# Attention and two feed-forward layers on one core: the hash codes' PSUM bank, maxima two slots earlier, weights in quarters

## The chip, the core and the metric

The kernel runs on one NeuronCore of a Trainium2 chip as a single program. The metric is device time in microseconds (us), the median of several executions. Engines are named as the profile names them: PE is the matrix engine (PEld its weight loads), DVE the vector engine, ACT the scalar engine, POOL GpSimd, SP the engine whose queue issues nearly all transfers.

## What is computed

Sixteen attention heads (2 batches of 8, 768 tokens, 64 columns each) in which a query sees only the keys with its own 6-bit hash code, then two layers over 1536 tokens of width 512 with 2048 hidden units.

```python
q_bits = (einsum('bhsd,dk->bhsk', q, proj) > 0); k_bits likewise
mask = q_bucket[:, :, :, None] == k_bucket[:, :, None, :]
scores = where(mask, scale * q @ k.T, -1e9)
attn = exp(scores - max(scores)); attn = attn / (sum(attn) + 1e-09)
x = (attn @ v) laid out as (1536, 512)
x = (mish(x @ w_in)) @ w_out
h = x @ w_in2;  P = a0 + a1*h + a2*h2 + a3*h3;  Q = 1 + |b0|*|h| + |b1|*h2
out = (P / (Q + 1e-06)) @ w_out2
```

## The kernel before

**Stages.** Attention comes first, head by head; the two layers follow (`moe`), whose matmuls on PE run without a break. What the change touches is all in `attention`.

**Slots.** Attention is written out by hand as a list of slots, six to a head: slot 6h + c holds, in the order of the table `order` (L506 to L533), every step due there. A row of the table is a name, a function, an offset and a count per head; `smax` at -9 means that the maxima of head h are taken from slot 6h - 9 on, one block c of 128 tokens in each slot. Steps before slot 0 are listed in `start` (L567), and steps after the last head are done within the first layer by `tail`. Every engine carries out its own instructions in this written order, so one that waits holds up all behind it on its engine; the same holds for the transfers that SP issues.

**A head's steps.** `load` brings k and q (`kq`, 64 rows each). `hi` (ACT) rounds them to the matrix engine's short format in `qB`, `lo` puts the remainder in `qX`, on POOL for even heads and DVE for odd ones. `move_k` copies k by a transfer (384 KB) from `qB` into both halves of `KK`. `move_x` issues two transfers, the second of which overwrites what the first reads, so SP waits in between. `codes` multiplies by the hash projection into a PSUM tile `cp`; `code_k` (DVE) and then `code_q` (ACT) turn it into 32 rows of `KK` and of `qB`. `code_q` overwrites rows of `qB` that `move_k` and `lo` read, so it waits for both. `smax` multiplies and takes each row's maximum on DVE (`mp`, L335); `fin_a` (three small DVE operations) and `fin_b` (four small transfers, two from SP and two from POOL) put the maxima back into `qB` as rows 29 to 31. `st` makes the scores (`sp`) and their exponentials `e` (ACT, L374). `pv` (`pv`) and `dsum` (`dn`) accumulate numerators and denominators in slots 3, 5 and 7; `evac` and `devac` copy them out, `recip`, `spread`, `norm`, `xhi` and `xlo` divide and split the result for the layers.

**PSUM.** Pool `ps` has three tiles, shared by `sp`, `mp`, `cp` and a small `vsp`; each is taken again once its reader is done. `pv` and `dn` have a bank each.

**Weights.** Meanwhile DVE turns 64-bit weights into 32-bit ones (`convert`, L100 to L106), POOL and DVE split the first five blocks, and the results go to DRAM; `first` reads each of these five blocks back in one transfer of 1024 KB (L143) at slots 80, 68, 74, 50 and 56.

Of the kernel before, what the change touches and what calls it, by code (L numbers as in the profile page):

```python
# [9 lines left out]
F32 = mybir.dt.float32  # L10
# [3 lines left out]
ACT = mybir.ActivationFunctionType  # L14
# [4 lines left out]
B, H, S, D = 2, 8, 768, 64  # L19
NT, DM, DFF = B * S, H * D, 2048  # L20
# [5 lines left out]
NC = S // 128  # L26
BIG = 2.0 ** 40
NBITS = 6
EARLY, FIRST = 5, (80, 68, 74, 50, 56)
SPLIT1, HERE1, W_AT, W_LEAD = 5, 10, (1, 7, 13, 19, 21), 3  # L30
DVE_LO = (("lo", 0),)
ENG = dict(
    lo="pd", hi="aa", xhi="a", xlo="pp", whi="pppp", wlo="pdpp",
)
C_AT = 16
ROW = 29
# [8 lines left out]
def attention_moe_moe(ctx: ExitStack, tc: tile.TileContext, kq, v, proj2, cst, eye, w1, w2, ab, out):  # L45
    nc = tc.nc

    def pool(stack, name, bufs=1, **kw):
        return stack.enter_context(tc.tile_pool(name=name, bufs=bufs, **kw))
# [111 lines left out]
    def attention(actx, tctx):  # L161
# [3 lines left out]
        dr_p = pool(tctx, "dr", 2, space=bass.MemoryType.DRAM)  # L165
        ac = pool(actx, "ac")
        kq_p = pool(actx, "kq")
        e_p = pool(actx, "pe", 5)
        v_p = pool(actx, "vp")
        sm_p = pool(actx, "sm", 2)  # L170
        ring[0] = pool(actx, "ring0", RING[0])
        ps = pool(actx, "ps", 3, space=PSUM)
        pvp = pool(actx, "pv", 1, space=PSUM)
# [11 lines left out]
        KK = [kq_p.tile([128, 2, S], R32, tag=f"kk{i}", name=f"kk{i}") for i in range(4)]  # L185
# [20 lines left out]
        raws = {}  # L206
# [21 lines left out]
        def lo(h, fn=None):  # L228
            if 0 <= h < B * H:
                fn = fn or lo_of("lo", h)  # L230
                fn(qX[h % 4], raws[h], qB[h % 4])

        def move_k(h):
            if 0 <= h < B * H:
                nc.sync.dma_start(
                    out=f32(KK[h % 4])[64:128], in_=f32(qB[h % 4])[0:64].unsqueeze(1).broadcast_to((64, 2, S))
                )

        def move_x(h):
# [55 lines left out]
        ct = {}  # L295


        def codes(h):
            if not 0 <= h < B * H:
                return  # L300
            ct[h] = ps.tile([128, 2, 512], F32, tag="s", name="cp")[:, 0]
            both(ct[h], p_raw, raws[h], start=True, stop=True)

        def code_k(h):
# [96 lines left out]
        Rt = {}  # L401
# [26 lines left out]
        def recip(h):
            if not 0 <= h < B * H:
                return  # L430
            cs = Rt.pop(h)
            rc = cs_p.tile([24, 32], F32, tag="rc", name="rc")

# [42 lines left out]
        nh = B * H  # L476
# [10 lines left out]
        for n, p in enumerate(parts):  # L487
            i = n // 5 * 24 + W_AT[n % 5]
# [6 lines left out]
                    if f is fn:  # L495
                        fn(0, *p)

        def first(f):
            (slot_both if wide64 else slot_f32)(0, f, lambda f: wpool)
            if not wide64:  # L500
                for s in range(2):
                    slot_hi(0, f, s)
                    slot_lo(0, f, s, lo_pool)
# [1 line left out]

        order = (  # L506
            ("st", st, 0, 6),
            ("smax", smax, -9, 6),
            ("fin_a", fin_a, -3, 1),
            ("fin_b", fin_b, -3, 1),  # L510
            ("hi", hi, -16, 1),
            ("move_k", move_k, -16, 1),
            ("lo", lo, -15, 1),
            ("codes", codes, -13, 1),
            ("pv", pv, (3, 3, 5, 5, 7, 7), 6),
            ("dsum", dsum, (3, 3, 5, 5, 7, 7), 6),
            ("vsum", vsum, 1, 0),
            ("code_k", code_k, -13, 1),
            ("code_q", code_q, -13, 1),
            ("evac", evac, 7, 1),  # L520
            ("devac", devac, 7, 1),
            ("recip", recip, 10, 1),
            ("spread", spread, 11, 1),
            ("norm", norm, 20, 0),
            ("xhi", xhi, 21, 0),
            ("vred", vred, -3, 0),
            ("xlo", xlo, 22, 0),
            ("move_x", move_x, -9, 1),
            ("load", load, -31, 1),
            ("load_v", load_v, -8, 0),  # L530
            ("weights", weights, 0, -1),
            ("first", first, FIRST, -2),
        )  # L533
        last = 6 * nh + 3
        slots = {}
        done = set()
        for name, fn, at, per in order:
            if name == "first":
                todo = [(at[f], (f,)) for f in range(EARLY)]
            elif type(at) is tuple:  # L540
                todo = [(at[c] + 6 * h, (h, c)) for h in range(nh) for c in range(per)]
            elif per > 0:
# [24 lines left out]
        start = (  # L567
            ("load", 0), ("get", 0), ("get", 1), ("hi", 0), ("codes", 0), ("move_k", 0), ("load", 1),
            ("lo", 0), ("get", 2), ("code_q", 0), ("code_k", 0), ("move_x", 0), ("smax", 0, 0), ("load", 2),
            ("smax", 0, 1), ("hi", 1), ("smax", 0, 2), ("codes", 1), ("move_k", 1), ("lo", 1), ("smax", 0, 3),  # L570
            ("load_v", 0), ("code_q", 1), ("smax", 0, 4), ("smax", 0, 5), ("fin_a", 0), ("fin_b", 0), ("code_k", 1),
            ("load", 3), ("move_x", 1), ("hi", 2), ("smax", 1, 0), ("coef",), ("move_k", 2), ("smax", 1, 1),
        )
# [305 lines left out]
```

## Time and profile before

| what | us |
|---|---|
| median of 3 runs (838.44 to 840.56) | 840.41 |
| the profiled execution | 841.66 |
| its span, first to last instruction | 839.1 |
| first scores (head 0 begins) | 23.30 |
| first matmul of the layers | 310.8 |

PE is busy for 790.9 us of the span, DVE for 589.3, ACT for 417.7. Head h is taken here from its first score matmul to that of head h + 1: they begin at 23.30, 45.83, 62.73, 78.79, 95.75, 117.35, 133.58, 149.71, 165.99, 189.21, 206.74, 222.75, 241.06, 263.12, 283.58 and 296.82 us. In a window's row PEclk is the granted TensorE clock as a share of the full one: 1.00 is 2.4 GHz, and a stretch at 1.2 GHz pulls the mean down. In a timeline's row the time in brackets is how long the engine stood idle before, and what ended that. A matmul's length overlaps the next one's, so PE's pace is read from start to start.

### The profile page before, as it was taken

What the parts mean: (1) busy time and instruction counts of PE and PEld (TensorE: products, weight loads), DVE (VectorE), ACT (ScalarE), POOL (GpSimd) and SP (SyncE); (2) the same over time, 40 slices, a digit from 0 to 9 for tenths busy, and PEclk for the clock granted to TensorE, in tenths of its full rate; (3) what the DMA queues carried; (4) which work ended last, traced back from release to release, by engine and by line L of the source; (5) the groups of instructions that cost most, each with busy time, mean ns of one, the idle gap of its engine ahead of it and who ended that gap; (6) DMA issues with size and microseconds to landing.
All of it is one profiled execution on the core that took longest, in us unless ns stands there. A gap on an engine that the chain in (4) does not pass through costs nothing.

```text
span 839.1 us, 10890 instructions
## 1 busy us (share of the span) xinstructions
PE 790.9 (94%) x3760; PEld 579.9 (69%) x3760; DVE 589.3 (70%) x1075; ACT 417.7 (50%) x680; POOL 84.6 (10%) x119
## 2 busy tenths in 40 slices
PE   4889899978988899999999999999999999999998
PEld 2545455445544458888888888887788888888886
DVE  4666657765664637865665567756999898889886
ACT  2245355444534354432222233337887777667674
POOL 2330415322030210000000000000000000000000
PEclk9899899999989899999999999999999999999999
DMA  5556665667655436332454468851000010001001
GB/s 133 171 133 164 173 163 162 177 173 186 180 149 155 131 99 220 92 109 89 148 169 159 140 180 267 238 176 55 1 1 0 13 38 0 1 1 51 0 1 50
DMA packets 58903, 95.41 MB, mean 114 GB/s; under 512 B 20866, under 2 KB 29154, under 8 KB 58210
## 3 DMA queue, kind: packets, MB, share of 16 engines
q1 hardware_dynamic: 57826, 94.65, 39.2%
q8 instruction: 29, 0.48, 0.2%
q0 software_dynamic: 1024, 0.09, 0.1%
q14 instruction: 24, 0.20, 0.1%
HBM read 62.43 MB, written 19.45 MB: 98 GB/s over the span
## 4 chain that ended last, share of the span: by engine, by line
PE 79%; DVE 8%; DMA 7%; ACT 2%; issue 2%; SPq 2%; POOL 0%; ACTq 0%; DVEq 0%
PE h L624 30%; PE y L642 15%; PE y L644 15%; PE sp L369 6%; PE pv L281 6%; DMA r<-w 4%; PE mp L331 3%; PE dn L396 3%; DVE m L335 3%; DMA kk<-qX 2%; DVE kk L308 1%; PE cp L281 1%; ACT qB L317 1%; DVE rc L434 1%; SPq L219 1%
## 5 line engine op out<-in xcount | busy, mean ns | idle before, releaser
L624 PE MATMUL h<-xh,w 128*128 128x512 f32 x768 | 204.9, 389 | 0.0
L624 PEld LDWEIGHTS h<-xh,w 128*128 128x128 f32 x768 | 144.2, 188 | 30.6 <-issue 0.6
L335 DVE TENSOR_REDUCE m<-mp 128x1 f32<-128x768 f32 x96 | 89.8, 945 | 51.1 <-PE mp L331 50.7
L70 DVE TENSOR_TENSOR gl<-ep,gh 128x512 fp32r<-128x512 f32 x96 | 67.1, 699 | 72.5 <-ACT ep L668 71.7
L374 ACT ACTIVATE e<-sp 128x768 f32<-128x768 f32 x96 | 77.3, 810 | 66.9 <-PE sp L369 63.6
L667 ACT ACTIVATE gh<-h 128x512 fp32r<-128x512 f32 x48 | 28.7, 598 | 162.3 <-PE h L624 153.5
L624 PE MATMUL h<-xl,w 128*128 128x512 f32 x384 | 102.7, 389 | 0.0
L644 PE MATMUL y<-w,gh 128*128 128x512 f32 x384 | 96.3, 389 | 0.0
L642 PE MATMUL y<-gh,w 128*128 128x512 f32 x384 | 94.8, 389 | 0.0
L642 PEld LDWEIGHTS y<-gh,w 128*128 128x128 f32 x384 | 72.1, 188 | 15.0
L644 PEld LDWEIGHTS y<-w,gh 128*128 128x128 f32 x384 | 72.1, 188 | 14.9
L624 PEld LDWEIGHTS h<-xl,w 128*128 128x128 f32 x384 | 72.1, 188 | 15.0
L281 PE MATMUL pv<-e,vf 128*64 128x384 f32 x384 | 77.0, 525 | 0.0
L369 PE MATMUL sp<-qB,kk 128*128 128x384 f32 x192 | 58.3, 386 | 18.7 <-DMA qB<-stt 5.1
L331 PE MATMUL mp<-kk,qB 128*128 128x384 f32 x192 | 58.3, 392 | 14.0 <-DVE kk L308 7.6
L369 PEld LDWEIGHTS sp<-qB,kk 128*128 128x128 f32 x192 | 32.1, 197 | 51.8 <-issue 25.9
L100 DVE TENSOR_SCALAR t<-r 128x256 int32<-128x256 int32 (+1 forms) x108 | 33.8, 313 | 47.3 <-DMA r<-w 46.0
L331 PEld LDWEIGHTS mp<-kk,qB 128*128 128x128 f32 x192 | 36.4, 210 | 26.6 <-DVE m L335 10.2
L674 ACT ACTIVATE ep<-h 128x512 f32<-128x512 f32 x48 | 28.6, 595 | 52.3 <-PE h L624 52.3
L106 DVE SCALAR_TENSOR_TENSOR r<-r,t 128x256 int32<-128x256 int32 (+1 forms) x108 | 51.2, 474 | 4.2
L103 DVE SCALAR_TENSOR_TENSOR t<-r,t 128x256 int32<-128x256 int32 (+1 forms) x108 | 51.3, 475 | 3.7
L644 PE MATMUL y<-w,gl 128*128 128x512 f32 x192 | 53.3, 392 | 0.5 <-DVE gl L70 0.4
(78 smaller groups left out, 1049.7 us busy)
## 6 DMA issues: line engine op xcount, KB each, us to landing
r<-w SPq DMA_DIRECT2D x88, 256.0 KB
w<-w SPq DMA_DIRECT2D x21, 512.0 KB
r<-w SPq DMA_DIRECT2D x20, 512.0 KB
w<-r SPq DMA_DIRECT2D x64, 128.0 KB
w<-r SPq DMA_DIRECT2D x30, 256.0 KB
kq<-kq SPq DMA_DIRECT2D x16, 384.0 KB
kk<-qB SPq DMA_DIRECT2D x16, 384.0 KB
w<-w SPq DMA_DIRECT2D x5, 1024.0 KB
```

The lines of the kernel that those rows point to most:

```text
L70: nc.vector.tensor_tensor(out=o, in0=i, in1=f32(h), op=ALU.subtract)
L100: lambda: nc.vector.tensor_scalar(out=t, in0=r[:, :, 1], scalar1=3, scalar2=0x3FFFFFF8, op0=ALU.logical_shift_left, op1=ALU.bitwise_and),
L103: lambda: nc.vector.scalar_tensor_tensor(out=t, in0=r[:, :, 1], scalar=-0x40000000, in1=t, op0=ALU.bitwise_and, op1=ALU.bitwise_or),
L106: lambda: nc.vector.scalar_tensor_tensor(out=o, in0=r[:, :, 0], scalar=29, in1=t, op0=ALU.logical_shift_right, op1=ALU.bitwise_or),
L281: nc.tensor.matmul(out=o[64 * a:64 * a + 64, 0:HALF], lhsT=w, rhs=qhalf(x, a), start=start, stop=stop)
L331: nc.tensor.matmul(out=p[:, a, 0:HALF], lhsT=qB[h % 4][:, c * 128:(c + 1) * 128], rhs=qhalf(KK[h % 4][:, 0], a), start=True, stop=True,)
L335: nc.vector.tensor_reduce(out=mt[h][:, c:c + 1], in_=halves(p), op=ALU.max, axis=AX.XY)
L369: nc.tensor.matmul(out=p[:, a, 0:HALF], lhsT=kk[:, c * 128:(c + 1) * 128], rhs=qq[:, a * HALF:(a + 1) * HALF], start=(i == 0), stop=(i == 1),)
L374: nc.scalar.activation(out=wide(e), in_=halves(p), func=ACT.Exp, scale=1.0 / D ** 0.5)
L624: nc.tensor.matmul(out=p, lhsT=w[:, c * 128:(c + 1) * 128], rhs=x[:, c, :], start=(n == 0), stop=(n == 11))
L642: nc.tensor.matmul(out=y[m], lhsT=w[:, DM + m * 128:DM + (m + 1) * 128], rhs=g, **s)
L644: nc.tensor.matmul(out=y[m], lhsT=g[:, m * 128:(m + 1) * 128], rhs=w[:, DM:2 * DM], **s)
```

## The change

- `codes` takes its tile from the denominators' pool (tag `dn`) instead of `ps`, and moves from offset -13 to -16, with `code_k`; `code_q` goes to -15. For the bank to be free then, `dsum` does its first group in slot 5 together with the second, and the pool of exponentials `e` grows from 5 to 6.
- `smax` goes from -9 to -11, `fin_a` and `fin_b` from -3 to -5, `hi` and `lo` to -18, `move_k` to -17; head 1 has a denser plan of its own.
- `move_x` is cut into `move_x` (-14) and `move_h` (-12); `devac`, `recip` give their transfers to `gather` (one slot later) and `store` (one slot later); `spread`, `norm`, `xhi`, `xlo` follow one to two slots later.
- `lo` is on POOL for all heads, `xlo` on DVE.
- `first` reads each of the five blocks in four transfers of 256 KB, two slots apart. Conversions move by two slots, their loads are issued four slots ahead instead of three.
- For head 0, `khi` (ACT) makes both copies of k from `kq`; the transfer `move_k` is not issued there.

```diff
-EARLY, FIRST = 5, (80, 68, 74, 50, 56)
-SPLIT1, HERE1, W_AT, W_LEAD = 5, 10, (1, 7, 13, 19, 21), 3
+EARLY, FIRST = 5, (84, 68, 76, 52, 60)
+SPLIT1, HERE1, W_AT, W_LEAD = 5, 10, (3, 9, 15, 17, 21), 4
-    lo="pd", hi="aa", xhi="a", xlo="pp", whi="pppp", wlo="pdpp",
+    lo="pp", hi="aa", xhi="a", xlo="dd", whi="pppp", wlo="pdpp",
-        e_p = pool(actx, "pe", 5)
+        e_p = pool(actx, "pe", 6)
+        def khi(h, i):
+            nc.scalar.activation(out=KK[h % 4][64:128, i], in_=raws[h][0:64], func=ACT.Copy)
...
-            ct[h] = ps.tile([128, 2, 512], F32, tag="s", name="cp")[:, 0]
+            ct[h] = pvp.tile([128, 512], F32, tag="dn", name="cp")
...
+        def first(f, n):
+            if wide64:
+                if n == 0:
+                    slot(0, f, lambda f: wpool)
+                c = slice(n // 2 * DM, (n // 2 + 1) * DM)
+                nc.sync.dma_start(out=f32(W[0, f])[:, n % 2, c], in_=scr[0, f][:, n % 2, c])
...
-            ("smax", smax, -9, 6),
+            ("smax", smax, -11, 6),
...
-            ("codes", codes, -13, 1),
+            ("codes", codes, -16, 1),
...
-            ("dsum", dsum, (3, 3, 5, 5, 7, 7), 6),
+            ("dsum", dsum, (5, 5, 5, 5, 7, 7), 6),
```

What this does to the engines' programs shows at three places. First PE in head 1, before: `sp` are scores, `mp` maxima, `cp` codes, `pv` and `dn` numerators and denominators.

```order
L369 MATMUL sp<-qB_122,kk_130 128x384 x2
L369 MATMUL sp<-qX_126,kk_130 128x384 x2
L331 MATMUL mp<-kk_132,qB_124 128x384 x2
L281 MATMUL cp<-kq,pr 64x384 x2
L281 MATMUL pv<-e,vf_133 64x384 x4
L396 MATMUL dn<-e,ones 32x384 x4
L369 MATMUL sp<-qB_123,kk_131 128x384 x2
```

The codes stand in the head's last slot, just ahead of a `pv` group. Now the same head after the change, from its third slot to its fifth.

```order
L337 MATMUL mp<-kk_132,qB_124 128x384 x2
L287 MATMUL cp<-kq,pr 64x384 x2
L375 MATMUL sp<-qB_122,kk_130 128x384 x2
L375 MATMUL sp<-qX_126,kk_130 128x384 x2
L337 MATMUL mp<-kk_132,qB_124 128x384 x2
L293 MATMUL pv<-qB_122,vs_136 128x384 x2
L287 MATMUL pv<-e,vf_133 64x384 x4
L375 MATMUL sp<-qB_122,kk_130 128x384 x2
L375 MATMUL sp<-qX_126,kk_130 128x384 x2
L337 MATMUL mp<-kk_132,qB_124 128x384 x2
```

The codes now follow the third slot's maxima, the fourth slot's `pv` has no `dn` behind it, and the sixth slot ends with eight `dn` matmuls in the bank that the codes had.

Second, SP's queue in the same head, before: `kk<-qB` is `move_k`, `qB<-stt` is `fin_b`, `kk<-qX` and `qX<-qB` are `move_x`, `cs`, `d` and `R` belong to the division.

```order
L423 DMA cs<-dv 24x1x32 x2
L235 DMA kk_129<-qB_121 64x2x768
L138 DMA w_0_306<-r 128x512
L139 DMA w_0_306<-r 128x512
L355 DMA qB_123<-stt_117 3x6x32 x2
L241 DMA kk_132<-qX_128 64x768
L242 DMA qX_128<-qB_124 64x768
```

After the change the two transfers of `fin_b` come directly ahead of `move_k`:

```order
L248 DMA qX_128<-qB_124 64x768
L361 DMA qB_123<-stt_117 3x6x32 x2
L238 DMA kk_129<-qB_121 64x2x768
L435 DMA cs<-dv 24x1x32 x2
L244 DMA kk_129<-qX_125 64x768
L138 DMA w_0_364<-r 128x512
```

So `move_k` of head 4 stands on SP behind the maxima of head 2, which DVE has to finish first; `move_x` is no longer followed by the transfer that waits for it.

Third, ACT round `code_q` (L317 before, L323 after), before:

```order
L412 ACTIVATE ev<-pv 64x384 x2
L420 ACTIVATE dv<-dn 128x384
L374 ACTIVATE e<-sp 128x768
L61 ACTIVATE qB_121<-kq 128x768
L374 ACTIVATE e<-sp 128x768 x3
L317 ACTIVATE qB_121<-cp,cst 32x384 x2
```

and after:

```order
L61 ACTIVATE qB_121<-kq 128x768
L380 ACTIVATE e<-sp 128x768
L418 ACTIVATE ev<-pv 64x384 x2
L426 ACTIVATE dv<-dn 128x384
L380 ACTIVATE e<-sp 128x768 x2
L323 ACTIVATE qB_121<-cp,cst 32x384 x2
```

Between `hi` (L61) and `code_q` there were three exponentials' time; there are now three exponentials and the two copies `ev` and `dv`, and `move_k` starts a slot later.

## Rows read from the trace of the kernel before

**Rows 1.** Windows: stretch, length, busy per engine (count), PEclk, DMA share, GB/s.

```profile
23.30:45.83 22.53, 19.17 (x82) 12.00 (x83) 13.21 (x22) 7.19 (x10) 5.02 (x8) 0.85 0.60 166
45.83:95.75 49.92, 46.33 (x276) 25.76 (x273) 34.48 (x59) 24.67 (x38) 12.95 (x16) 1.00 0.60 162
95.75:117.35 21.60, 18.42 (x96) 9.90 (x92) 14.26 (x28) 8.50 (x13) 8.04 (x11) 0.84 0.51 140
117.35:165.99 48.64, 46.18 (x277) 25.70 (x273) 32.98 (x57) 25.58 (x40) 18.77 (x20) 1.00 0.67 178
165.99:283.58 117.59, 99.78 (x546) 54.68 (x542) 71.03 (x131) 50.61 (x77) 26.98 (x36) 0.93 0.64 166
283.58:310.80 27.22, 27.22 (x176) 14.47 (x172) 13.12 (x27) 13.68 (x22) 3.12 (x4) 1.00 0.36 114
310.80:839.08 528.28, 523.80 (x2308) 432.18 (x2304) 398.03 (x737) 281.38 (x474) 2.36 (x2) 1.00 0.28 87
```

**Rows 2.** Waits of PE, whole span: us in total, times, longest.

```profile
PE mp L331 <- DVE kk L308: 7.6, 2, 5.0
PE mp L331 <- DVE m L335: 6.3, 8, 1.8
PE cp L281 <- ACT e L374: 5.3, 10, 0.6
PE sp L369 <- DMA qB<-stt: 5.1, 3, 2.2
PE sp L369 <- ACT qB L317: 4.7, 3, 2.0
PE sp L369 <- DVE m L335: 4.3, 5, 1.1
```

**Rows 3.** Timeline of the start: start us, length, instruction, [idle before, releaser].

```profile
4.72 0.74 SPq L235 DMA_DIRECT2D kk<-qB  x1
...
8.69 1.16 ACT L317 ACTIVATE qB<-cp,cst 32x384 fp32r<-32x384 f32 x2 [3.99 <-DMA kk<-qB]
9.95 1.37 DVE L308 TENSOR_SCALAR kk<-cp,cst 32x384 fp32r<-32x384 f32 x2 [4.27 <-ACT qB L317]
...
10.72 2.63 PE L331 MATMUL mp<-kk,qB 128*128 128x384 f32 x6 [5.03 <-DVE kk L308]
...
12.67 0.62 SPq L235 DMA_DIRECT2D kk<-qB  x1
...
18.20 1.16 ACT L317 ACTIVATE qB<-cp,cst 32x384 fp32r<-32x384 f32 x2 [6.62 <-DMA kk<-qB]
...
23.30 0.98 PE L369 MATMUL sp<-qB,kk 128*128 128x384 f32 x2 [1.15 <-issue]
```

**Rows 4.** Timeline where head 8 begins: VectorE, GpSimd, ScalarE and PE.

```profile
163.62 1.83 POOL L67 TENSOR_TENSOR qX<-kq,qB 128x768 fp32r<-128x768 f32 x1
...
164.37 2.09 DVE L434 TENSOR_TENSOR rc<-cs 24x32 f32<-24x32 f32 x1
...
168.27 0.62 PE L331 MATMUL mp<-kk,qB 128*128 128x384 f32 x2 [1.30 <-DVE m L335]
...
170.87 1.01 PE L369 MATMUL sp<-qB,kk 128*128 128x384 f32 x2 [1.98 <-ACT qB L317]
```

**Rows 5.** Timeline round a weight transfer of 1024 KB, between heads 12 and 13.

```profile
253.69 1.25 SPq L143 DMA_DIRECT2D w<-w  x1
...
255.04 1.56 SPq L355 DMA_DIRECT2D qB<-stt  x2
...
263.12 0.59 PE L369 MATMUL sp<-qB,kk 128*128 128x384 f32 x2 [1.62 <-DMA qB<-stt]
```

**Rows 6.** Timeline of PE at the end of head 4, a quiet place.

```profile
114.48 0.87 PE L281 MATMUL cp<-kq,pr 128*64 128x384 f32 x4 [0.43 <-ACT e L374]
...
116.57 0.85 PE L396 MATMUL dn<-e,ones 128*32 128x384 f32 x8
...
117.35 0.62 PE L369 MATMUL sp<-qB,kk 128*128 128x384 f32 x2
```

More of the change, by code (lines that the diff above doesn't have):

```diff
@@ L241, in move_x, with move_h @@
                 nc.sync.dma_start(out=f32(KK[h % 4])[0:64, 1], in_=f32(qX[h % 4])[0:64])
+        def move_h(h):
+            if 0 <= h < B * H:
                 nc.sync.dma_start(out=f32(qX[h % 4])[0:64], in_=f32(qB[h % 4])[64:128])
@@ L420, in devac, with gather @@
             nc.scalar.activation(out=dv, in_=pvt.pop((h, "d"))[:, 0:HALF], func=ACT.Copy)
+            Rt[h] = dv
+        def gather(h):
+            if not 0 <= h < B * H:
+                return
+            dv = Rt.pop(h)
             cs = cs_p.tile([24, 2, 32], F32, tag="cs", name="cs")
@@ L439, in recip, with store @@
             nc.vector.reciprocal(out=rc, in_=rc)
+            Rt[h, "r"] = rc
+        def store(h):
+            if not 0 <= h < B * H:
+                return
+            rc = Rt.pop((h, "r"))
             d = dr_p.tile([24, 32], F32, tag="d", name="d")
@@ L496, in weights @@
                         fn(0, *p)
-        def first(f):
-            (slot_both if wide64 else slot_f32)(0, f, lambda f: wpool)
-            if not wide64:
+        def first(f, n):
[4 more added lines that the diff above has]
+                nc.sync.dma_start(out=f32(W[0, f])[:, n % 2, c], in_=scr[0, f][:, n % 2, c])
+            elif n == 3:
+                slot_f32(0, f, lambda f: wpool)
                 for s in range(2):
@@ L507, in attention @@
             ("st", st, 0, 6),
-            ("smax", smax, -9, 6),
[L509 to L513, printed above, removed]
-            ("codes", codes, -13, 1),
+            ("smax", smax, -11, 6),
+            ("fin_a", fin_a, -5, 1),
+            ("fin_b", fin_b, -5, 1),
+            ("hi", hi, -18, 1),
+            ("move_k", move_k, -17, 1),
+            ("lo", lo, -18, 1),
+            ("codes", codes, -16, 1),
             ("pv", pv, (3, 3, 5, 5, 7, 7), 6),
-            ("dsum", dsum, (3, 3, 5, 5, 7, 7), 6),
+            ("dsum", dsum, (5, 5, 5, 5, 7, 7), 6),
             ("vsum", vsum, 1, 0),
-            ("code_k", code_k, -13, 1),
-            ("code_q", code_q, -13, 1),
+            ("code_k", code_k, -16, 1),
+            ("code_q", code_q, -15, 1),
             ("evac", evac, 7, 1),
             ("devac", devac, 7, 1),
+            ("gather", gather, 8, 1),
             ("recip", recip, 10, 1),
[L523 to L528, printed above, removed]
+            ("store", store, 11, 1),
+            ("spread", spread, 12, 1),
+            ("norm", norm, 22, 0),
+            ("xhi", xhi, 23, 0),
+            ("xlo", xlo, 24, 0),
+            ("vred", vred, -5, 0),
+            ("move_x", move_x, -14, 1),
+            ("move_h", move_h, -12, 1),
             ("load", load, -31, 1),
-            ("load_v", load_v, -8, 0),
+            ("load_v", load_v, -10, 0),
             ("weights", weights, 0, -1),
@@ L538, in attention @@
             if name == "first":
-                todo = [(at[f], (f,)) for f in range(EARLY)]
+                todo = [(at[f] + 2 * n, (f, n)) for f in range(EARLY) for n in range(4)]
             elif type(at) is tuple:
                 todo = [(at[c] + 6 * h, (h, c)) for h in range(nh) for c in range(per)]
+            elif name == "smax":
+                todo = [(c // 2 if h == 1 else at + 6 * h + c, (h, c)) for h in range(nh) for c in range(per)]
+            elif name.startswith("fin_"):
+                todo = [(at + 6 * h + (h == 1), (h,)) for h in range(nh)]
             elif per > 0:
@@ L567, in attention @@
         start = (
[L568 to L572, printed above, removed]
+            ("load", 0), ("get", 0), ("get", 1), ("hi", 0), ("codes", 0), ("khi", 0, 0), ("lo", 0), ("load", 1),
+            ("code_q", 0), ("code_k", 0), ("khi", 0, 1), ("get", 2), ("move_x", 0), ("smax", 0, 0), ("hi", 1),
+            ("smax", 0, 1), ("move_k", 1), ("load", 2), ("lo", 1), ("smax", 0, 2), ("codes", 1), ("move_h", 0),
+            ("smax", 0, 3), ("smax", 0, 4), ("smax", 0, 5), ("fin_a", 0), ("fin_b", 0), ("code_k", 1), ("code_q", 1),
+            ("load_v", 0), ("move_x", 1), ("load", 3), ("hi", 2), ("move_k", 2), ("smax", 1, 0), ("coef",),
+            ("move_h", 1), ("smax", 1, 1),
         )
@@ L577, in run @@
             fns = {o[0]: o[1] for o in order}
-            fns.update(get=get, coef=coef)
+            fns.update(get=get, coef=coef, khi=khi)
             for name, *k in start:
-                done.add((name, tuple(k)))
+                done.add(("move_k" if name == "khi" else name, tuple(k[:1]) if name == "khi" else tuple(k)))
                 fns[name](*k, **({"fn": lo_dve} if (name, *k) in DVE_LO else {}))
@@ L585, in tail @@
         def tail(i):
-            for g in {1: range(last, last + 3), 3: range(last + 3, last + 6), 4: range(last + 6, last + 30)}.get(i, ()):
+            for g in {1: range(last, last + 3), 2: range(last + 3, last + 5), 4: range(last + 5, last + 30)}.get(i, ()):
                 slot_ops(g)
```

## The prediction

> **What bounds the kernel now.** I read the windows first. The layers take 528.28 us from their first matmul on, 523.80 of them with PE busy at a clock of 1.00 [rows 1]; no step of the change runs there except the ends of the last pair's division, so I carry this stretch over unchanged. The room is in the 310.8 us before it. There the heads differ: heads 5 to 7 take 48.64 us, 16.2 each, heads 1 to 3 take 16.6 each, but head 0 takes 22.5, head 4 takes 21.6, and heads 8 to 13 take 117.59, which is 19.6 each [rows 1]. All do the same work, so what they take above 16.2 is waiting and a lower clock: 6.3 + 1.3 + 5.4 + 20.4 = 33.4 us. The clock's part shows in PEclk: 0.84 over the 21.60 us of head 4 means (1 - 0.84)/0.5 x 21.6 = 6.9 us at 1.2 GHz instead of 2.4, which costs up to half of that, 3.5 us; every window with PEclk under 1.00 is one with long heads. Heads 14 and 15 (27.22 us) have next to no maxima or codes left to do.
>
> Next the waits of PE. Its six largest sums are 7.6, 6.3, 5.3, 5.1, 4.7 and 4.3 us, together 33.3 [rows 2]. The first belongs mostly to the start. PE, then, is the bound in the quiet heads, and in the others it stands behind short chains of other engines.
>
> Two places show these chains. Where head 8 begins, POOL's 1.83-us `lo` starts at 163.62; a DVE operation on only 24x32 elements that starts 0.75 us later takes 2.09 us; the maxima queue behind it on DVE, PE waits 1.30 us for one, the codes' readers come late too, and PE waits 1.98 us more because the tile that its next scores want still holds the codes (`ACT qB L317`) [rows 4]. Between heads 12 and 13, a transfer of 1024 KB is issued at 253.69, the maxima's two small ones 1.35 us later, and PE gets them only at 263.12, after a wait of 1.62 us [rows 5].
>
> **The change part by part.**
>
> *Start.* ACT stands idle for 3.99 us until 8.69 because `code_q` overwrites rows that the transfer `move_k` reads (issued at 4.72) [rows 3]. `khi` puts a pass of ACT over 768 columns there; the two passes of `code_q`, 384 columns each, take 1.16 together [rows 3], so I price it at 0.8 to 1.2. The wait shrinks by 2.8 to 3.2 us, and the second copy stands behind `code_q`, with no one waiting. `code_k` and the first maxima (10.72) follow as before. Term: -3.0. Head 0's scores then begin near 20.
>
> *Codes' bank.* `cp` no longer waits for an exponential (5.3 us in 10 waits) and scores no longer wait for `code_q` (4.7 us in 3) [rows 2]; in a quiet head this is the 0.43 before `cp` [rows 6]. The new wait is for `devac`, one slot earlier; it is the last of three ACT copies behind `pv` and `dn`, and has a slot's scores and maxima as cover. If that cover is gone it costs what it cost before, about half a microsecond a head. `cp` itself (114.48 to 115.18 with what follows, 0.70) only moves. The merged `dn` group is the same matmuls (0.78 from start to start [rows 6]) and go to the sum as they are.
>
> *Maxima two slots earlier.* The 5.1 us behind `qB<-stt` go: two slots are about a third of a head, 5.4 us, against a lateness of 1.62 in the case shown. What is late next is `code_q`, below.
>
> *Weights in quarters.* The 1024 KB that stood in front of small transfers becomes 256 KB at a time. Bounds: nothing, or all of what heads 8 to 13 have above the quiet ones. SP issues 15 transfers more; at 1.25 us, the longest row I have [rows 5], that is 19 us of a queue spread over six heads (96 us), and it is hidden as long as SP waits for others anyway.
>
> *`lo` to POOL, `xlo` to DVE; loads four slots ahead; `gather`, `store`, `move_h`.* Eight `lo` against seven or eight pairs' `xlo` is an exchange of equal size, off PE's path. The division's new place takes `recip` away from `lo`, so the case of rows 4 goes, and with it most of the 6.3 + 4.3 us behind DVE's maxima. But it puts `lo` of every head beside `fin_a`. The last pair's `norm` now ends two slots later, inside the first layer; the columns that it makes are first used 16 blocks in. A sixth `e` tile costs only memory.
>
> The Trainium skill ("SBUF — State Buffer", section "Who interferes with whom") says that DVE and GpSimd hold one pair of ports as an exclusive lock for a whole instruction, and that the later one fully blocks. The 2.09 us of rows 4 agree in kind. By this rule `fin_a` (operations from SBUF to SBUF) would wait for the rest of each `lo`, at most its 1.83 us, per head; that is a delay on the chain priced next, and no wait of PE by itself.
>
> *The new chain.* `code_q` waits for `move_k` to land, and `move_k` now stands behind `fin_b` on SP, which stands behind `fin_a`. From issue to `code_q`'s start it took 3.97 us (4.72 to 8.69) and 5.53 (12.67 to 18.20) [rows 3]. Behind it, `code_q` takes 1.16, then `dn` may have its bank. So the chain from `fin_a` is 1.56 for two issues [rows 5], 4.0 to 5.5, and 1.16: 6.7 to 8.3 us, or up to 10.1 with a `lo` of 1.83 in front. From the second slot, where it begins, to the sixth, where `dn` wants the bank, are four of six slots, 4/6 x 16.2 = 10.8 us. So it just fits: I take no wait in most heads. In the two heads where a weight's split stands in the same slot on POOL and SP, `move_k` is delayed by it further, and I expect a wait of 1.5 to 2 us and a stretch of low clock (3.5) each, some 10 us in all. Queued behind `code_q` on ACT are the exponentials of slots 4 and 5, for which the next head's first scores wait.
>
> *Sum.* Start -3.0. Head 0, denser than before, 20.5 instead of 22.5: -2.0. Heads 1 to 13 at 15.7 (16.2 less the 0.53 of one `cp` wait): 13 x 15.7 = 204, plus the 10 us of new waits, 214, against 49.92 + 21.60 + 48.64 + 117.59 = 237.8: -23.7. Heads 14 and 15 and the layers: 0. Together -28.7, so the profiled execution's 841.66 would be 813.0. It stands 1.25 us above the median of the runs shown (840.41); from that median the forecast is 811.7, and I say **812 us**.
>
> **Range of the forecast's own case.** Without the 10 us and with head 0 at 17.5, -42: 798. With half of the excess of heads 8 to 13 left (10) on top of the new waits, -19: 822.
>
> **The rivals.**
>
> *Only the bank and the start* (disturbed heads stay). The unknown is whether quarters and earlier maxima cure heads 8 to 13. For: the same number of bytes still passes, beside the same loads. Against: each long wait there had a named cause that the change moves away. It keeps 3.0 + 5.3 + 4.7 = 13 us, so 827; with the wait for maxima also gone, 822.
>
> *The new chain is late in every head* (slower). If `move_k` needs more than 10.8 - 1.83 - 1.56 - 1.16 = 6.2 us from issue to landing, PE waits at `dn` in each head, ACT's exponentials follow late, and the clock falls. Price: a wait of 2 us in 13 heads and a low stretch of 3.5 after every second, 26 + 24 = 50 us, against 38.7 that are gained without new waits: +11, so 852. It decides from 38.7/13 = 3.0 us a head on. For it: the sum of the longest rows fits by 0.7 us only, and weights' quarters pass at the same time. Against: the other row, 3.97, leaves 2.2.
>
> *The bank is not free* (the change doesn't do what it says). `cp` waits for `devac` as it waited for the exponential. Then heads 1 to 13 stay at 16.2: 6.9 us less, 819.
>
> **How the numbers follow.** Forecast's case 0.62 (798 to 822), only bank and start 0.16, bank not free 0.08, a chain late in some heads that eats nearly all of the gain 0.05 (about 840), late in all 0.09. Within 0.3%, which is 2.5 us and about what a measurement of this kernel can tell from no change, lies the fourth. Faster by more 0.86, same 0.05, slower 0.09. The range leaves out the two last cases and a little at the low end: 799 to 831.
>
> **What would show it.** Right: first scores near 20 us; no row in which PE's `cp` waits for `e` or `sp` for `code_q`; heads 8 to 13 under 17 us each; at most two or three stretches at the low clock. Wrong: PE's `dn` waiting for ACT's `code_q`, and ACT's `code_q` for the transfer `kk<-qB`, in many heads; the last `fin_a` operation stretched to the end of POOL's `qX` and PE behind it; PE idle in the first blocks of the layers, because a weight's last quarter or the last division comes late.

## The result

| kernel | median, us | ratio to before | 95% interval |
|---|---|---|---|
| before | 839.42 | | |
| changed | 808.93 (808.24 to 808.95, 4 runs) | 0.9636 | 0.9616 to 0.9656 |

The forecast was 812, with 799 to 831. The kernel before and its variants scatter by about 1% either way, so for them I go by the ratio, which leaves disturbed runs out; the changed kernel's runs agree within 0.1%.

The profile after, windows over the same groups of heads as [rows 1] (stretch, length, busy per engine with counts, PEclk, DMA share, GB/s):

```profile
19.78:44.14 24.36, 19.77 (x88) 11.83 (x87) 15.05 (x24) 7.91 (x11) 8.47 (x9) 0.77 0.79 200
44.14:92.66 48.52, 45.75 (x276) 25.97 (x272) 37.63 (x63) 24.77 (x38) 17.93 (x21) 1.00 0.66 177
92.66:108.72 16.06, 15.62 (x97) 8.73 (x93) 13.67 (x24) 8.16 (x13) 5.06 (x5) 1.00 0.64 169
108.72:156.32 47.60, 46.03 (x276) 25.89 (x272) 38.60 (x64) 24.87 (x39) 20.76 (x23) 1.00 0.71 189
156.32:251.05 94.73, 91.38 (x546) 51.77 (x542) 70.85 (x127) 50.13 (x78) 22.57 (x26) 1.00 0.68 187
251.05:277.16 26.11, 26.11 (x172) 14.04 (x168) 12.01 (x29) 13.59 (x22) 1.32 (x2) 1.00 0.51 150
277.16:806.90 529.74, 524.08 (x2308) 432.11 (x2304) 397.78 (x739) 281.89 (x474) 0.00 (x0) 1.00 0.28 87
```

Head 4 takes 16.06 us where it took 21.60; heads 8 to 13 take 94.73 instead of 117.59, and PEclk is 1.00 in every window from head 1 on. Of these stretches of heads only head 0's has become longer, 24.36 instead of 22.53, at a PEclk of 0.77. Put into the prediction's sum:

| term | forecast | measured | from |
|---|---|---|---|
| start, to the first scores | -3.0 | -3.5 | 23.30 to 19.78 |
| head 0 | -2.0 | +1.8 | 22.53 to 24.36 |
| heads 1 to 13 | -23.7 | -30.8 | 237.75 to 206.91 |
| heads 14 and 15 | 0 | -1.1 | 27.22 to 26.11 |
| layers | 0 | +1.5 | 528.28 to 529.74 |
| sum | -28.7 | -32.2 | span 839.08 to 806.90 |

The waits of PE, of ACT and of DVE on which the rest turns (us in total, times, longest):

```profile
PE mp L337 <- ACT qB L323: 6.5, 2, 4.1
PE mp L337 <- DVE m L341: 5.7, 11, 1.5
PE mp L337 <- DVE kk L314: 2.3, 1, 2.3
PE dn L402 <- ACT qB L323: 0.3, 1, 0.3
...
ACT qB L323 <- DMA kk<-qB: 25.3, 11, 4.1
...
DVE t L100 <- DMA r<-w: 18.7, 13, 4.3
```

Of [rows 2], the lines in which `cp` waits for `e`, `sp` for `code_q` and `sp` for `qB<-stt` are gone. The new chain is there, as the ACT line shows: `code_q` stands behind `move_k`'s transfer 11 times for 25.3 us. But PE pays 0.3 us for it at `dn`, once; the 6.5 us before `mp` lie ahead of head 0's first scores and in head 0 (below).

So the total came out, and the symptom that it rested on (long heads become quiet ones) is what happened. Which part of the change does it, the prediction had argued only from single waits. That is what the experiments ask.

### The profile page after: what moved, and what is told of

It is laid out like the page before. It is cut to its first block, busy times and chain, and to the rows that moved or that the text cites. A ratio compares the mean times of both kernels' runs of the same rounds, so it can differ in the third digit from the quotient of the medians.

```text
span 806.9 us, 10904 instructions
## 1 busy us (share of the span) xinstructions
PE 778.0 (96%) x3760; PEld 575.8 (71%) x3760; DVE 595.3 (74%) x1083; ACT 419.1 (52%) x682; POOL 83.7 (10%) x111
## 3 DMA queue, kind: packets, MB, share of 16 engines
q0 software_dynamic: 1024, 0.09, 0.1%
## 4 chain that ended last, share of the span: by engine, by line
PE 78%; DVE 12%; DMA 2%; ACT 2%; issue 1%; SPq 0%; POOL 0%; DVEq 0%; ACTq 0%; POOLq 0%
PE h L656 29%; PE y L676 15%; PE y L674 14%; PE pv L287 6%; PE sp L375 6%; PE dn L402 4%; DVE m L341 4%; PE mp L337 3%; DMA r<-w 2%; DVE w L70 1%; DVE kk L314 1%; DVE t L103 1%; DVE xl L70 1%; DVE r L106 1%; DVE t L100 1%
## 5 line engine op out<-in xcount | busy, mean ns | idle before, releaser
L699 ACT ACTIVATE gh<-h 128x512 fp32r<-128x512 f32 x48 | 28.7, 598 | 150.8 <-PE h L656 141.8
L287 PE MATMUL pv<-e,vf 128*64 128x384 f32 x384 | 72.5, 499 | 0.0
L337 PE MATMUL mp<-kk,qB 128*128 128x384 f32 x192 | 55.7, 381 | 16.6 <-ACT qB L323 6.5
L375 PE MATMUL sp<-qB,kk 128*128 128x384 f32 x192 | 56.6, 376 | 0.5 <-ACT e L380 0.5
L708 DVE TENSOR_TENSOR n<-n,ep 128x512 f32<-128x512 f32 x48 | 33.1, 690 | 26.7 <-ACT n L707 26.7
```

The costliest lines, as they stand in the source:

```text
L337: nc.tensor.matmul(out=p[:, a, 0:HALF], lhsT=qB[h % 4][:, c * 128:(c + 1) * 128], rhs=qhalf(KK[h % 4][:, 0], a), start=True, stop=True,)
L375: nc.tensor.matmul(out=p[:, a, 0:HALF], lhsT=kk[:, c * 128:(c + 1) * 128], rhs=qq[:, a * HALF:(a + 1) * HALF], start=(i == 0), stop=(i == 1),)
L708: nc.vector.tensor_tensor(out=v_, in0=v_, in1=u, op=ALU.mult)
```

## The experiments

First the changed kernel with single parts undone. Three undo kernels that change nothing measurable (below) gave 808.15 to 808.28 us, and the changed kernel itself 808.93, so I take 808.5 us as the reference for all of them.

### Weights in one transfer each

```diff
-                if n == 0:
-                    slot(0, f, lambda f: wpool)
-                c = slice(n // 2 * DM, (n // 2 + 1) * DM)
-                nc.sync.dma_start(out=f32(W[0, f])[:, n % 2, c], in_=scr[0, f][:, n % 2, c])
+                if n == 0:
+                    slot_both(0, f, lambda f: wpool)
```

> The changed kernel (808.9 us), but each of the five weight blocks comes back in one transfer of 1024 KB, at the slot where its first quarter stood. Theory (quarters carry a part of their own): move_k, now 3.5 to 3.8 us from issue to landing in the middle heads, lands behind 1024 KB only after 6 to 8 us in the heads that have such a transfer; code_q follows late, PE waits at dn or mp, and the clock falls in some of them: 6 to 15 us slower (815 to 824), the excess in heads 8 to 15. Rival (the earlier maxima give enough slack by themselves, the quarters are not needed): late landings show on SP and ACT, but PE hardly waits: 807 to 811.

Measured: 808.28 us (808.21 to 808.65), ratio 0.9666 (0.9625 to 0.9708). The rival holds: cutting the blocks is worth nothing.

### Maxima back at their old place

```diff
-            ("smax", smax, -11, 6),
-            ("fin_a", fin_a, -5, 1),
-            ("fin_b", fin_b, -5, 1),
+            ("smax", smax, -9, 6),
+            ("fin_a", fin_a, -3, 1),
+            ("fin_b", fin_b, -3, 1),
```

> The changed kernel, but the maxima at -9 and fin_a, fin_b at -3 as before. Theory (the quarters already cured the late maxima): fin_b lands 1.9 to 2.9 us after its issue now and has three slots, about 8 us, before the scores want it, so PE waits for qB<-stt nowhere, and the time is 807 to 811. Rival (the two slots carry the gain of heads 8 to 13): the 5.1 us of waits behind qB<-stt come back with one to three stretches of low clock, 815 to 824.

Measured: 808.26 us (807.89 to 809.6), ratio 0.9668 (0.9626 to 0.9711). No scores wait for `qB<-stt` anywhere. The earlier maxima are not needed either.

### Both of these undone at once

> The changed kernel with both undone at once: weight blocks in one transfer each, and the maxima at -9 with fin_a, fin_b at -3. Each alone left the time at 808.3. Theory A (each covers for the other: early maxima stand the long transfer, quarters let late maxima pass): undone together, the waits for qB<-stt of before come back in heads 8 to 13, with low clock, 814 to 822. Theory B (neither carries anything; what disturbed heads 4 and 8 to 13 was the codes in the pool ps and lo beside recip): 806.5 to 811.

Measured: 808.15 us (807.55 to 809.22), ratio 0.9623 (0.9592 to 0.9653). They don't cover for each other; theory B holds against theory A. One reservation: the blocks stand here in the new slots. Before, all five stood one slot ahead of `fin_b`, and in its trace POOL's small transfers issued 1.4 to 3.2 us behind a block landed 5.5 to 7.2 us after their issue, all others in 1.7 to 4.0. In this kernel only one block stands there. But the place isn't needed either: a kernel below (the one before with bank and conversions) has the blocks whole and in their old slots and the maxima at -9, and in it too no scores wait for `qB<-stt`.

### Codes back in the pool of the scores

```diff
-            ct[h] = pvp.tile([128, 512], F32, tag="dn", name="cp")
+            ct[h] = ps.tile([128, 2, 512], F32, tag="s", name="cp")[:, 0]
```

> The changed kernel, but the codes take their tile from the pool ps again, in the new slots. Theory (the bank carries about 10 us): scores and maxima wait again until code_q has read the tile, and code_q now waits for move_k in most heads, so the waits are longer than the 5.3 + 4.7 us of before: 10 to 25 us slower, 819 to 834, with PE rows sp or mp waiting for code_q. Rival (the bank only moves a wait): within 2.5 us, 806.5 to 811.5.

Measured: 818.87 us (818.83 to 820.65), ratio 0.9799 (0.9748 to 0.9851), 10.4 us slower than the reference, at the low end of what the theory said. PE's waits in this kernel:

```profile
PE sp L375 <- DVE m L341: 7.7, 7, 1.4
...
PE sp L375 <- ACT qB L323: 5.5, 6, 1.1
```

Scores wait for `code_q` again, six times, and for maxima whose tiles come free later; neither row exists after the change. The clock stays at 1.00 in heads 1 to 13, which take 215.78 us instead of 206.91.

### `lo` and `xlo` back on their engines

```diff
-    lo="pp", hi="aa", xhi="a", xlo="dd", whi="pppp", wlo="pdpp",
+    lo="pd", hi="aa", xhi="a", xlo="pp", whi="pppp", wlo="pdpp",
```

> The changed kernel, but lo on DVE for odd heads and xlo on POOL, as before. Theory (an exchange of equal size off PE's path): 807 to 811; the first fin_a operation of the heads whose lo is now on DVE is back at 0.16 us from 1.1. Rival (the exchange matters): lo and fin_a now queue on DVE in the same slot ahead of maxima, PE waits for m in every second head by up to 1 us, and the time is 812 to 818.

Measured: 805.34 us (805.16 to 806.06), ratio 0.9632 (0.959 to 0.9673). Neither theory: undoing this part is 3.2 us *faster*. The changed kernel's timeline shows where, the first three rows in head 6, the last in head 1 (start, length, instruction):

```profile
126.50 2.68 DVE L70 TENSOR_TENSOR xl<-xf,xh 128x512 fp32r<-128x512 f32 x2
126.88 2.01 POOL L67 TENSOR_TENSOR qX<-kq,qB 128x768 fp32r<-128x768 f32 x1 [5.03 <-ACT qB L61]
129.10 0.94 DVE L341 TENSOR_REDUCE m<-mp 128x1 f32<-128x768 f32 x1
...
47.53 1.08 DVE L348 TENSOR_SCALAR smt<-m 128x12 fp32r<-128x12 f32 x1
```

Of the two `xl` operations the first takes 0.68 us and the second, which starts beside POOL's `lo`, 2.08; this happens in heads 4, 6, 8 and 10, and the maxima behind it come late. Those heads take 16.1 us each; with `lo` on DVE there and `xlo` on POOL they take 15.7, which is 1.5 of the 2.7 us by which heads 1 to 13 become shorter; the rest of the gain, in heads 2, 7 and 12 and 1.4 us in the layers, is not traced. The last line shows that the first operation of `fin_a` stretches as well (0.16 us where POOL is idle), in heads 1, 2, 5, 7 and 9 and in part in 11 and 12; heads 1, 5 and 9, at 15.54, are nevertheless the shortest up to head 12.

The Trainium skill ("SBUF — State Buffer", section "Who interferes with whom") says that a DVE instruction with two SBUF inputs contends with a GpSimd instruction that reads SBUF. The 2.08 us of `xl` agree. The prediction had applied the page to `fin_a`, whose first operation has one input only: it did stretch, to the end of POOL's `lo`, and cost nothing that the heads show. It had not applied it to `xlo`, where it cost.

### Head 0 by transfer

```diff
-            ("load", 0), ("get", 0), ("get", 1), ("hi", 0), ("codes", 0), ("khi", 0, 0), ("lo", 0), ("load", 1),
-            ("code_q", 0), ("code_k", 0), ("khi", 0, 1), ("get", 2), ...
+            ("load", 0), ("get", 0), ("get", 1), ("hi", 0), ("codes", 0), ("move_k", 0), ("lo", 0), ("load", 1),
+            ("code_q", 0), ("code_k", 0), ("get", 2), ...
```

> The changed kernel, but k of head 0 is copied by the transfer move_k, not by ACT. Theory (the start's term): code_q of head 0 waits again for the transfer, the first maxima come 2.7 to 3.0 us later (10.7 instead of 8.0), the first scores 2.7 to 3.5 later, and the time is 811 to 813. Rival (what is won there is lost again in head 0, which stands behind code_q of heads 1 and 2): the first scores are later, head 0 shorter by as much, 807.5 to 810.

Measured: 811.55 us (811.13 to 812.22), ratio 0.9662 (0.9633 to 0.9692): 3.0 us slower, as the theory said. PE's first wait for `code_k` is that of [rows 3] again:

```profile
PE mp L337 <- DVE kk L314: 5.0, 1, 5.0
```

### The bank alone, and the conversions

With 3.0 us for the start and 10.4 for the bank, some 17 us of the gain have no part to belong to. So the other way round: the kernel before, with the bank and only the moves that it needs.

```diff
-            ct[h] = ps.tile([128, 2, 512], F32, tag="s", name="cp")[:, 0]
+            ct[h] = pvp.tile([128, 512], F32, tag="dn", name="cp")
...
-            ("codes", codes, -13, 1),
+            ("codes", codes, -16, 1),
...
-            ("dsum", dsum, (3, 3, 5, 5, 7, 7), 6),
+            ("dsum", dsum, (5, 5, 5, 5, 7, 7), 6),
```

> The kernel before with the codes' bank alone and what it needs: cp from the denominators' pool, hi and lo at -18, move_k at -17, codes and code_k at -16, code_q at -15, the merged dn group, six e tiles. Start, maxima, weights, loads and division as before. Theory B (the bank with these moves carries the gain of heads 1 to 13): 812 to 818, heads 8 to 13 under 17 us each. Theory A (heads 8 to 13 need earlier maxima or quarters as well): those heads stay at 18 to 20 us, 822 to 830.

Measured: 842.54 us, ratio 1.0066 (1.0038 to 1.0094). Both theories fall: the bank alone makes the kernel a little slower, and every second head from 3 to 11 takes 21 to 22 us. `cp` no longer waits for `e`, nor `sp` for `code_q`, but the waits for maxima grew from 6.3 + 4.3 us [rows 2] to

```profile
PE sp L369 <- DVE m L335: 17.5, 9, 3.1
...
PE mp L331 <- DVE m L335: 9.0, 9, 3.2
...
DVE t L100 <- DMA r<-w: 58.0, 23, 5.9
```

The last line points at a cause: DVE stands for 58.0 us at the first operation of a weight conversion, for its load from memory. One such place, in the order of time:

```profile
231.48 0.83 SPq L119 DMA_DIRECT2D r<-w  x1
...
237.94 0.43 DVE L100 TENSOR_SCALAR t<-r 128x512 int32<-128x512 int32 x1 [4.38 <-DMA r<-w]
...
239.74 0.95 DVE L335 TENSOR_REDUCE m<-mp 128x1 f32<-128x768 f32 x1
...
242.85 0.96 DVE L335 TENSOR_REDUCE m<-mp 128x1 f32<-128x768 f32 x1
...
243.86 0.97 PE L369 MATMUL sp<-qB,kk 128*128 128x384 f32 x2 [2.49 <-DVE m L335]
```

A load is late: DVE comes to it 2.1 us after its issue and stands 4.38 us, the maxima whose matmuls PE has done lie behind the conversion, and when DVE has worked its way through PE has stood 2.49 us. The same line of the kernel before, over the whole span and up to the layers:

```profile
DVE t L100 <- DMA r<-w: 46.0, 18, 6.2
DVE t L100 <- DMA r<-w: 33.6, 9, 6.2
```

Some 12 to 17 us of each total fall into the layers. Up to them it is 41.8 us in 11 with the bank alone, and 4.6 in 2 in the changed kernel, in heads 14 and 15. I had taken DVE's waits there for harmless, as idle time of an engine that is not the bound. New theory (C): the conversions' new slots and the longer lead of their loads, which the prediction listed among the edits without a price, carry much of the gain.

Undone in the changed kernel:

```diff
-SPLIT1, HERE1, W_AT, W_LEAD = 5, 10, (3, 9, 15, 17, 21), 4
+SPLIT1, HERE1, W_AT, W_LEAD = 5, 10, (1, 7, 13, 19, 21), 3
```

> The changed kernel, but the conversions of weights in their old slots and their loads three slots ahead, as before. Theory C (what carries heads 4 and 8 to 13 is that a conversion's load is there when DVE comes to it; DVE waits for r<-w 18.7 us in 13 in the changed kernel, 46.0 in 18 before, 58.0 in 23 in the run with the bank alone, where PE then waits 26.5 us behind DVE's maxima): DVE's wait for r<-w rises to over 40 us, PE waits for m, the clock falls in some heads, 818 to 835. Theory D (the old places do harm only with SP's queue as it was, where move_x waits between its two transfers and the loads stand behind): the loads are issued in time anyway, 807 to 812.

Measured: 822.42 us (820.68 to 824.0), ratio 0.9813 (0.9754 to 0.9871): 14 us slower, as theory C says: 5.9 in head 0, 8.0 in heads 1 to 13. DVE's wait is 33.3 us in 16, less than the 40 that I expected, but it falls where it hurts. Up to head 13 there are three such waits, 5.29 us in head 0, 1.47 in head 7 and 3.00 in head 11; PE then stands 4.00, 2.33 and 3.76 us for maxima, and these are the heads that become long: 30.27, 19.15 and 20.57 us instead of 24.36, 15.93 and 16.23. So the theory has the mechanism right but not the heads: head 4 and heads 8 to 10 stay quiet. In head 11:

```profile
218.56 0.50 SPq L469 DMA_DIRECT2D R<-d  x1
...
219.75 0.59 SPq L119 DMA_DIRECT2D r<-w  x1
...
226.95 0.43 DVE L100 TENSOR_SCALAR t<-r 128x512 int32<-128x512 int32 x1 [3.00 <-DMA r<-w]
...
228.75 0.95 DVE L341 TENSOR_REDUCE m<-mp 128x1 f32<-128x768 f32 x1
...
229.75 0.62 PE L337 MATMUL mp<-kk,qB 128*128 128x384 f32 x2 [3.76 <-DVE m L341]
```

The load stands on SP behind a step of the division (`R<-d`, which waits 66.3 us in 16 on SP in this kernel, 23.7 in 14 in the changed one) and lands 7.1 us after its issue. DVE comes to it after 4.2 us, waits the other 3.00, and PE stands 3.76. In the changed kernel DVE comes to the same load (the 15th) 7.8 us after its issue and doesn't wait; to its first 18 loads it comes 6.8 to 11.6 us after their issue and waits for none:

```profile
206.07 0.35 SPq L119 DMA_DIRECT2D r<-w  x1
...
213.91 0.42 DVE L100 TENSOR_SCALAR t<-r 128x512 int32<-128x512 int32 x1
```

The line holds two things, the conversions' slots and the lead of their loads; they were not tried apart. The same line of code, put into the kernel with the bank alone:

> The kernel before with the codes' bank and its moves (842.5 us so), and the conversions' new slots with loads four slots ahead. Theory C: DVE's wait for r<-w falls under 30 us, heads 8 to 13 take under 17 us each, 811 to 820. Theory D (SP's queue has to be changed too: move_h, gather, store): DVE still waits over 40 us, every second head stays at 21 us, 830 to 845.

Measured: 823.02 us (821.3 to 825.37), ratio 0.9823 (0.9773 to 0.9873), some 20 us faster than without it. DVE's wait is 26.1 us in 21, 9.6 in 6 of it up to the layers. Theory C holds in kind. But heads 2, 6 and 9 still take 19 to 22 us, and PE's waits for `m` are 20.9 us in 13, so the time is above what C said for its end (811 to 820): the rest of the change is worth something too.

Last, the line alone in the kernel before:

> The kernel before with the conversions' new slots and loads four slots ahead alone (with the bank as well it was 823.0 us, with the bank alone 842.5). Theory (the two add up: each takes away waits of its own): DVE's wait for r<-w falls from 46.0 to under 30 us, but PE's waits for exponentials and code_q on account of the codes in ps stay, about 10 us: 826 to 834. Rival 1 (the lead does it all here, the bank nothing while SP's queue is the old one): 820 to 825. Rival 2 (the lead helps only once the bank has moved the codes): 836 to 842.

Measured: ratio 0.9925 (0.9874 to 0.9976), runs from 823.9 to 838.9, about 833 by the ratio; the profiled run 832.57. It lies in the range of the sum's theory, but the sum itself doesn't hold: alone, the bank is worth +0.7% and the conversions -0.8%, together -1.8%. In this kernel DVE's wait for `r<-w` is down to 20.1 us in 15 (6.1 in 5 up to the layers), but the waits of the codes are still there, and those for maxima are no shorter than before (6.3 + 4.3 us [rows 2]):

```profile
PE sp L369 <- DVE m L335: 8.3, 6, 2.4
...
PE sp L369 <- ACT qB L317: 7.5, 7, 2.0
PE mp L331 <- DVE m L335: 5.6, 4, 1.9
...
PE cp L281 <- ACT e L374: 4.3, 10, 0.4
```

Each of the two edits takes away one kind of wait, and PE then meets others. Both are needed, and together they bring 1.8 of the 3.6%, some 15 of the 30 us.

### Head 0

Why did head 0 become longer? The changed kernel's timeline of it:

```profile
17.71 1.18 ACT L323 ACTIVATE qB<-cp,cst 32x384 fp32r<-32x384 f32 x2 [8.91 <-DVE kk L314]
18.34 1.65 PE L337 MATMUL mp<-kk,qB 128*128 128x384 f32 x4 [4.07 <-ACT qB L323]
...
19.70 0.59 SPq L213 DMA_DIRECT2D kq<-kq  x1
...
25.00 0.84 ACT L61 ACTIVATE qB<-kq 128x768 fp32r<-128x768 f32 x1 [2.87 <-DMA kq<-kq]
...
26.86 1.18 ACT L323 ACTIVATE qB<-cp,cst 32x384 fp32r<-32x384 f32 x2 [1.03 <-DMA kk<-qB]
27.49 0.76 PE L337 MATMUL mp<-kk,qB 128*128 128x384 f32 x2 [2.38 <-ACT qB L323]
```

PE stands 4.07 us for `code_q` of head 1 and 2.38 for that of head 2. There are two stretches at 1.2 GHz, 6.8 us each: one begins at 17.6, inside the first wait, the other at 27.8, just behind the second. The new place of the maxima is not the reason by itself: with the maxima back at -9 head 0 took 24.88 us; PE stood 4.7 us for `code_q` ahead of it and 6.0 us in it, at `vsp` for POOL's `vsum`. I rearranged the start against these two waits.

```diff
-            ("smax", 0, 3), ("smax", 0, 4), ("smax", 0, 5), ("fin_a", 0), ("fin_b", 0), ("code_k", 1), ("code_q", 1),
-            ("load_v", 0), ("move_x", 1), ("load", 3), ("hi", 2), ("move_k", 2), ("smax", 1, 0), ("coef",),
-            ("move_h", 1), ("smax", 1, 1),
+            ("code_k", 1), ("code_q", 1), ("smax", 0, 3), ("smax", 0, 4), ("smax", 0, 5), ("fin_a", 0), ("fin_b", 0),
+            ("hi", 2), ("move_k", 2), ("load_v", 0), ("move_x", 1), ("load", 3), ("smax", 1, 0), ("coef",),
+            ("move_h", 1), ("smax", 1, 1), ("smax", 1, 2),
```

> The changed kernel, but in the list start code_k and code_q of head 1 stand before the last three maxima of head 0, move_k of head 2 directly behind fin_b, and the third maxima of head 1 ahead of the first scores. Theory (head 0 is long, 24.4 us, because PE stands 4.1 and 2.4 us behind code_q of heads 1 and 2 and the clock then falls twice, 13.6 us in all): both waits shrink to under 1 us, head 0 takes 18 to 21 us, and the time is 803 to 806. Rival (head 0 is limited by DVE's maxima and by the first loads, and the low clock comes anyway): the waits only change their names, 807 to 810.

Measured: 810.09 us (809.73 to 810.71), ratio 0.9645 (0.9615 to 0.9675): a miss, 1.6 us slower. Its timeline:

```profile
14.52 0.59 PE L337 MATMUL mp<-kk,qB 128*128 128x384 f32 x2 [0.36 <-ACT qB L323]
...
20.10 0.98 PE L375 MATMUL sp<-qB,kk 128*128 128x384 f32 x2 [3.28 <-DMA qB<-stt]
...
21.71 0.59 SPq L213 DMA_DIRECT2D kq<-kq  x1
...
26.55 0.84 ACT L61 ACTIVATE qB<-kq 128x768 fp32r<-128x768 f32 x1 [3.99 <-DMA kq<-kq]
27.42 1.18 ACT L323 ACTIVATE qB<-cp,cst 32x384 fp32r<-32x384 f32 x2
...
28.05 1.01 PE L337 MATMUL mp<-kk,qB 128*128 128x384 f32 x2 [3.14 <-ACT qB L323]
```

The first wait went (0.36), and another took its place: the maxima's own transfers, 3.28. The second was no matter of where `code_q` stands: on ACT, `hi` of head 3 stands ahead of it and waits 3.99 us for its load, which I had moved back by 2 us (from 19.70 to 21.71). So the last form loads head 3 right behind `move_h` of head 0, where SP has nothing to do, and takes `lo` and `xlo` back to their old engines.

```diff
-    lo="pp", hi="aa", xhi="a", xlo="dd", whi="pppp", wlo="pdpp",
+    lo="pd", hi="aa", xhi="a", xlo="pp", whi="pppp", wlo="pdpp",
...
-            ("smax", 0, 3), ("smax", 0, 4), ("smax", 0, 5), ("fin_a", 0), ("fin_b", 0), ("code_k", 1), ("code_q", 1),
-            ("load_v", 0), ("move_x", 1), ("load", 3), ("hi", 2), ("move_k", 2), ("smax", 1, 0), ("coef",),
-            ("move_h", 1), ("smax", 1, 1),
+            ("load", 3), ("load_v", 0), ("code_k", 1), ("code_q", 1), ("smax", 0, 3), ("smax", 0, 4), ("smax", 0, 5),
+            ("fin_a", 0), ("fin_b", 0), ("hi", 2), ("move_k", 2), ("move_x", 1), ("smax", 1, 0), ("coef",),
+            ("move_h", 1), ("smax", 1, 1), ("smax", 1, 2),
```

> The changed kernel with lo on DVE in odd heads and xlo on POOL (805.3 us so), and the start rearranged: kq of head 3 and v of the first pair are loaded right behind the first move_h, code_k and code_q of head 1 stand before the last three maxima of head 0, move_k of head 2 behind fin_b, the third maxima of head 1 ahead of the first scores. Theory (in the run with the start rearranged alone, 810.1 us, ACT stood 3.99 us at hi of head 3 for its load, issued at 21.71, with code_q of head 2 and the second exponential behind it; so PE stood 3.14 us): that wait goes, head 0 takes 18 to 21 us with at most one stretch of low clock, 798 to 803. Rival (the first maxima's transfers to the scores, 3.3 us of PE idle, and the low clock after it stay, and only they count): 804 to 807.

Measured: **802.62 us** (802.33 to 803.0), ratio 0.9578 (0.9532 to 0.9624), 6.3 us under the changed kernel. Windows of head 0 and of heads 8 to 13:

```profile
20.73:42.33 21.60, 20.28 (x84) 11.85 (x84) 13.62 (x22) 7.79 (x11) 5.46 (x8) 0.70 0.71 185
...
152.80:246.05 93.25, 90.93 (x546) 51.95 (x542) 67.61 (x125) 49.72 (x77) 22.99 (x31) 1.00 0.70 190
```

Head 0 is down to 21.60 us. Its PEclk is 0.70, lower than in the changed kernel: one stretch at 1.2 GHz, from 16.5 to 33.5, now covers most of it. PE's waits round its beginning:

```profile
15.28 1.29 PE L337 MATMUL mp<-kk,qB 128*128 128x384 f32 x4 [1.56 <-DVE m L341]
...
20.73 0.98 PE L375 MATMUL sp<-qB,kk 128*128 128x384 f32 x2 [2.91 <-DMA qB<-stt]
```

The clock falls between the two, behind 1.56 us for DVE's maxima and ahead of the 2.91 us for their transfers. Which of them to take away was not tried.

## Why the prediction was right, point by point

*What bounds the kernel.* Right: the room lay in the heads above 16.2 us and in their low clock, and the layers were carried over with an error of 1.5 us, 0.8 of it one wait of PE for `gl`.

*Start.* Right in size and in mechanism: -3.5 in the trace, 3.0 in the time when it is undone.

*Codes' bank.* Right that its waits go; the bank was free in time, and the rival in which it isn't didn't occur. The size, 10.4 us by the undo kernel against 5.3 + 4.7 read from [rows 2], agrees in part by luck, for the waits that come back there are in part others: 7.7 us for maxima and 5.5 for `code_q`, none of `cp` for `e`. What the prediction lacked is that the bank brings nothing where DVE is held up by its loads: with the moves that it needs, and nothing else, it is a loss of 0.7%. The rival *Only the bank and the start* counted the same 5.3 + 4.7 us, and in time the bank alone brings none of them.

*Maxima earlier, weights in quarters.* The step "the 5.1 us behind `qB<-stt` go" named the wrong cause. The waits went, but they go without either edit, and also with the blocks in their old slots. For the quarters I had left "nothing, or all" open; it is nothing.

*Loads four slots ahead.* This is the step that failed: in the prediction it stands in a heading among the exchanges, without a price, and together with the conversions' new slots it carries 14 us of the result. The row that would have shown it is DVE's wait for `r<-w` (33.6 us in 9 up to the layers), which I passed over because DVE isn't the bound; but it stands there in the order of its queue, with PE's maxima behind it. [rows 4] showed that kind of chain, for another operation. The size of DVE's wait alone would not have priced it: before, DVE stood 3.82 us for a load in head 5 and 3.39 in head 7, and both heads are quiet (16.2 and 16.3 us).

*`lo` and `xlo`.* "An exchange of equal size, off PE's path" was wrong by 3.2 us: `xlo` lies beside `lo`. Of the 6.3 + 4.3 us behind DVE's maxima, most of which was to go with `recip`'s new place, 5.7 are left. And in [rows 4] the 2.09-us operation ends at 166.46, 1.0 us after `lo`; POOL's next operation, `vsum`, runs from 165.39 to 166.41. So the 1.83 us of one `lo` were no upper bound for such a wait.

*The new chain.* Right that it exists and fits: `code_q` waits for `move_k` in 11 heads. The 10 us of new waits that I set aside for it came out at 0.3 (at `dn`). Without them heads 1 to 13 take 15.9 us each, 0.2 above the forecast's 15.7; so they beat it by 7 us. In the middle heads `move_k` took 3.7 to 4.1 us to land, nearer to the 3.97 of [rows 3] than to its 5.53.

*Head 0.* Mis-sized by 3.8 us: -2.0 forecast, +1.8 measured. I had no row for it. The denser plan put maxima of head 2 into head 0, and they stand behind `code_q`, which stands behind `hi` and a load; but head 0 stays as long without them (24.88 us with the maxima at -9), so what made it longer than before is only shown in part.

So the sum came within 3.1 us partly by luck, because the misses cancel in part: 7.1 us too little for heads 1 to 13, 3.8 too much for head 0. It was built on the right total, what the heads take above a quiet one, and that didn't depend on knowing which edit would bring it.

What stays open: between the kernel with bank and conversions (823.0) and the changed one lie some 14 us, of which the start is 3, and the exchange of `lo` and `xlo` takes 3.2 away. The rest may belong to the cut of `move_x` (SP waits 41.3 us between its two transfers in the former, 6.5 in the latter), to the division's later transfers and operations, to head 1's denser plan, or to the new slots of the blocks; they were not tried apart.

## What to carry to other kernels

Price an edit by undoing it, not by the wait that it was aimed at: here two of the parts that the title names were worth nothing, and a change of five numbers was worth 14 us. An engine's idle time is harmless only if nothing that the bound engine wants stands behind it in that engine's queue; so read for each wait of a side engine what comes next in its order. And where an engine's work is moved, look which operation of another engine it now lies beside.

## What was unexpected

- Two edits that were worth +0.7% and -0.8% alone gave -1.8% together.
- An `xl` operation on DVE, 0.68 us alone, took 2.05 to 2.08 us beside POOL's subtraction, which itself went from 1.83 to about 2.0.
- POOL's small transfers issued 1.4 to 3.2 us behind one of 1024 KB landed after 5.5 to 7.2 us instead of 1.7 to 4.0, yet cutting the 1024 KB into quarters changed the time by nothing.
